# A second product in twenty block products instead of Strassen's seven, with PSUM in one-bank tiles and part of a convolution on ScalarE and GpSimd

## The chip, the cores and the metric

The kernel runs on one core of a Trainium2 chip. The metric is device time in microseconds, the median of several runs. PE is TensorE, DVE is VectorE, ACT is ScalarE, POOL is GpSimd, SP the queue that issues most DMAs.

## The reference

x has shape (8, 4096, 192). Each of 8 heads (24 channels) is filtered along the sequence by 7 causal taps, the softmax of `weight`. The result, 32,768 tokens by 192, goes through an MLP of 2048 hidden units, all in float32:

```python
out = np.einsum('hk,bskhg->bshg', w, x_unf)      # 7 taps, per head
h = out.reshape(B * S, D) @ w_in                 # 192 -> 2048
g = h * (1.0 / (1.0 + np.exp(-1.702 * h)))
y = g @ w_out                                    # 2048 -> 192
```

## The kernel before

Work goes in 32 chunks (`big`), each of 512 tokens from both halves of the batch, 1024 in all. Channels or hidden units lie on the partitions, tokens along the free dimension. Chunk 0 goes its own way in `first_step`, beside loading, splitting and rounding the weights (which arrive as float64 words). Every later chunk is one step of three parts:

- The convolution on DVE, two chunks ahead: `transpose_x` (L414) turns x, `conv` (L429, L431) applies seven taps for each of three groups of 64 channels (c = 0, 1, 2), and `sums_c` (L338, L340) forms eight sums. DMAs copy them to the other half of the partitions (`cross`, L440).
- The first product, `hidden`, once for v = 0 and once for v = 1: 21 terms each, every term two matmuls of 512 columns on two row tiles side by side (L492). DVE and ACT combine the partial sums in PSUM and in `room`, and ACT applies the activation into `g` (`gelu`, L509).
- The second product, `output`: Strassen's scheme in Winograd's form, seven products of halves. Five calls of `product2` each give three column tiles of 32 to a product and the fourth to a third of another one; `quarters` (L614) does what is left. A product sums over 8 blocks of 128 hidden units, in matmuls of 512 columns (L597). DVE forms the sums of halves of g (`sum_1` to `sum_4`, L512), adds the products (L671 to L708) and transposes back (`turn`, L632). `store` (L645) writes out.

The order is written out by hand. `prepare` lists the convolution's operations, each with a cost in microseconds; `work(us)` takes as many off the list as fit, `need(label)` takes all up to a label:

```python
def work(us):
    while todo and todo[0][1] <= us + 0.2:
        us -= todo[0][1]
        todo.pop(0)[2]()
```

Every engine runs its own instructions in that order, semaphores between them. PSUM is four tiles of two banks each (`slots`, `sums`).

Of the kernel before, what the change touches and what calls it, by code (L numbers as in the profile page):

```python
# [8 lines left out]
F32 = mybir.dt.float32  # L9
# [6 lines left out]
def kernel(  # L16
# [44 lines left out]
    NK = NF // 2  # L61
# [15 lines left out]
    xin_pool = ctx.enter_context(tc.tile_pool(name="xin", bufs=1))  # L77
# [7 lines left out]
    xins, xts = {}, {}  # L85

    def load_x(big, ns=range(2)):
# [3 lines left out]
        if big not in xins:  # L91
            xins[big] = xin_pool.tile([P, 2, NJ, XW], F32, name="xin")
            if c == 0:
                nc.gpsimd.memset(xins[big][0:R, :, 0, :], 0.0)  # L94
        xin = xins[big]
# [14 lines left out]
    slots = [psum.tile([P, 2, TOK], F32, name=f"slot{i}") for i in range(3)]  # L110
    sums = psum.tile([P, 2, TOK], F32, name="sums")
# [3 lines left out]
    B11, B12, B21, B22, T1, T2 = range(6)  # L115
    T3, T4 = B12, B21
    g = consts.tile([P, 4, NU, 2, 2, TOK], F32)
# [4 lines left out]
    k15, k20, k19, k18, k16 = (room[:, i, :].rearrange("p (h n) -> p h n", h=2) for i in range(5))  # L122
    u1, u2 = (room[0 : NC * Q, 4, i * TOK : (i + 1) * TOK] for i in range(2))
    osbs = consts.tile([P, 4 * TOK], F32)
    osb = osbs[0 : NC * Q, :].rearrange("q (n j e) -> q n j e", n=2, e=2 * Q)
    p3, p4 = (osb[:, n, :, Q : 2 * Q] for n in (1, 0))

    def half(b, u, cols, small):


        if small and b in (T1, T2):
            return room[:, 2 * (b - T1) + u, :].rearrange("p (v h t) -> p v h t", v=2, h=2)
        if b == T2:
            t = room[:, 2 * u : 2 * u + 2, :].rearrange("p v (h t) -> p v h t", h=2)
        else:
            t = g[:, B11 if b == T1 else b, u, :, :, :]
        return t[:, :, :, cols]

# [59 lines left out]
    NS = 7  # L200
    A11, A12, A21, A22, S1, S2, S4 = range(NS)
    S3 = A21
    w_out_s = consts.tile([P, NS, NK, HD], F32)

# [6 lines left out]
    assert PIECE == CW * D and 3 * PIECE <= NB * T and 3 * PIECE <= 2 * NJ * XW  # L211
    flat_room = room.rearrange("p i n -> p (i n)")
    places = w_in_s[:, 4 * NC : NA, :].rearrange("p a f -> p (a f)")
    b12, b22 = (g[:, b, 1, :, :, :].rearrange("p v h t -> p (v h t)") for b in (B12, B22))
# [13 lines left out]
    def scratch(flat):  # L228
# [6 lines left out]
        scratch(w_out_s[:, S1 : S4 + 1, :, :].rearrange("p i f d -> p (i f d)")),  # L235
# [100 lines left out]
    def add_up(v, dst, a, op, b):  # L336
        if op == "+":
            vec.tensor_add(v(dst), v(a), v(b))  # L338
        elif op == "-":
            vec.tensor_sub(v(dst), v(a), v(b))  # L340
        elif op == "n":
            vec.scalar_tensor_tensor(
                out=v(dst), in0=v(a), scalar=-1.0, in1=v(b), op0=ALU.mult, op1=ALU.subtract
            )
        else:
            vec.tensor_scalar_mul(v(dst), v(a), -1.0)
# [10 lines left out]
    def round_w_out(i):  # L357
        join_piece(NW + i)
        k, j = divmod(i * CW, NK)
        round_piece(  # L360
            NW + i,
            [
                (
                    lambda v, m=m: v.rearrange("p (b m d) -> p b m d", m=2, d=Q)[:, :, m, :],
                    w_out_s[:, 2 * m + k, j : j + CW, :].rearrange("p j (c d) -> p (j c) d", d=Q),
                )
                for m in range(2)
            ],
        )

    def sums_w_out():
        a = [w_out_s[:, i, :, :] for i in range(NS)]
        vec.tensor_add(a[S1], a[A21], a[A22])
        vec.tensor_sub(a[S2], a[S1], a[A11])
        vec.tensor_sub(a[S4], a[A12], a[S2])
# [9 lines left out]
    pw = slots[0][:, 0, 0 : NC * (K + 1)].rearrange("p (c k) -> p c k", c=NC)  # L385


    def begin_sums(js, dst=sums):
        for j in js:
            nc.tensor.matmul(  # L390
                dst[:, j // 4, j % 4 * P : (j % 4 + 1) * P],
# [543 lines left out]
```

## Time and profile before

| | |
|---|---|
| median of 3 runs | 2353.68 us (2353.04 to 2353.89) |
| profiled execution, span from first to last instruction | 2351.6 us |
| granted TensorE clock, mean | 0.999 |
| busy PE, DVE, ACT, POOL | 2343.7, 1951.7, 1018.4, 5.8 us |
| SP queue's share of 16 DMA engines | 27.5% |

The profiled execution's own time is known only as its span; 2.1 us lie between it and the median. The profile lists groups of instructions by source line, with count, total busy time, mean duration and the idle time ahead of them. In the timeline a row has the start, the duration, and the count of instructions merged into it.

### The profile page before, as it was taken

Reading aid. Unit: us, or ns where it says so; the run is one execution under the profiler, and the core shown is the slowest. Engines: PE = TensorE matmul, PEld = TensorE weight load, DVE = VectorE, ACT = ScalarE, POOL = GpSimd, SP = SyncE. Lnnn points to the kernel's source line nnn. Section 1 sums busy time; section 2 is a strip of 40 time slices with the busy share of each in tenths; the row PEclk is TensorE's granted clock in tenths of the full one; section 3 lists DMA queues with packets and bytes.
Section 4 is the critical chain, followed back from the end, with each engine's and each line's share of the span. In section 5 each row is a group of like instructions: output and inputs, shape, how many; then the busy total and the mean of one; then the engine's idle time right before and its main releaser. Section 6 shows DMA issues by size and latency. Waiting matters only on the chain.

```text
span 2351.6 us, 39193 instructions
## 1 busy us (share of the span) xinstructions
PE 2343.7 (100%) x16856; PEld 892.0 (38%) x16856; DVE 1951.7 (83%) x2186; ACT 1018.4 (43%) x1159; POOL 5.8 (0%) x23
## 2 busy tenths in 40 slices
PE   9999999999999999999999999999999999999998
PEld 5533333333333333333333333333333333333333
DVE  8988888888888888888888888888888888888866
ACT  7234543345533355433454334543345533345433
POOL 0000000000000000000000000000000000000000
PEclk9999999999999999999999999999999999999999
DMA  8323313323123232132331332312323223231010
GB/s 182 69 48 76 68 21 64 63 57 68 36 49 66 55 69 50 35 65 55 68 64 22 68 64 58 68 30 54 67 55 69 46 39 67 55 68 43 17 41 15
DMA packets 197484, 133.67 MB, mean 57 GB/s; under 512 B 108592, under 2 KB 187824, under 8 KB 193344
## 3 DMA queue, kind: packets, MB, share of 16 engines
q1 hardware_dynamic: 196448, 130.92, 27.5%
q8 instruction: 132, 2.16, 0.4%
q14 instruction: 40, 0.33, 0.0%
q10 hardware_dynamic: 832, 0.20, 0.0%
q0 software_dynamic: 32, 0.07, 0.0%
HBM read 53.15 MB, written 25.17 MB: 33 GB/s over the span
## 4 chain that ended last, share of the span: by engine, by line
PE 67%; issue 32%; DMA 0%; DVE 0%; POOL 0%; POOLq 0%; DVEq 0%
PE slot L492 24%; PE slot L597 22%; PE sums L492 11%; PE sums L597 9%; PE slot L614 1%; PE slot L740 0%; PE sums L390 0%; DMA conv_t<-conv_t 0%; DVE xt L414 0%; PE slot L401 0%; POOLq L930 0%; POOL xin L94 0%; PE slot L390 0%; POOL osbs masks.py:199 0%; POOL osbs masks.py:197 0%
## 5 line engine op out<-in xcount | busy, mean ns | idle before, releaser
L492 PE MATMUL slot<-conv_t,w_in_s 64*128 64x512 f32 x3740 | 851.8, 590 | 0.0
L597 PE MATMUL slot<-g,w_out_s 128*32 128x512 f32 (+2 forms) x6864 | 788.7, 568 | 0.0
L492 PEld LDWEIGHTS slot<-conv_t,w_in_s 64*128 64x128 f32 x3740 | 359.6, 187 | 446.8 <-issue 394.6
L431 DVE SCALAR_TENSOR_TENSOR conv_t<-xt,cw,conv_t 128x512 f32<-128x512 f32 (+1 forms) x576 | 424.8, 738 | 13.0
L597 PEld LDWEIGHTS slot<-g,w_out_s 128*32 128x32 f32 x6864 | 241.8, 110 | 455.9 <-issue 439.0
L492 PE MATMUL sums<-conv_t,w_in_s 64*128 64x512 f32 x1660 | 405.4, 592 | 0.0
L509 ACT ACTIVATE g<-room 128x1024 f32<-128x1024 f32 x310 | 321.1, 1058 | 97.5 <-DVE room L574 58.3
L597 PE MATMUL sums<-g,w_out_s 128*32 128x512 f32 (+1 forms) x2304 | 335.0, 587 | 0.0
L512 DVE TENSOR_TENSOR g<-g 128x2048 f32<-128x2048 f32 (+1 forms) x126 | 283.2, 2267 | 4.7 <-PE sums L597 2.4
L492 PEld LDWEIGHTS sums<-conv_t,w_in_s 64*128 64x128 f32 x1660 | 158.3, 187 | 202.9 <-issue 160.9
L509 ACT ACTIVATE g<-slot 128x1024 f32<-128x1024 f32 x167 | 169.4, 1016 | 88.7 <-PE slot L492 88.7
L597 PEld LDWEIGHTS sums<-g,w_out_s 128*32 128x32 f32 x2304 | 93.1, 110 | 152.7 <-issue 146.3
L512 DVE TENSOR_TENSOR room<-g 128x2048 f32<-128x2048 f32 (+1 forms) x64 | 144.6, 2259 | 4.3
L512 DVE TENSOR_TENSOR g<-room,g 128x2048 f32<-128x2048 f32 (+1 forms) x64 | 140.2, 2229 | 0.0
L685 ACT COPY osbs<-slot 32x512 f32<-32x512 f32 (+1 forms) x32 | 18.3, 572 | 251.6 <-PE slot L614 251.6
L597 PE MATMUL slot<-room,w_out_s 128*32 128x512 f32 (+1 forms) x816 | 112.9, 567 | 0.0
L597 PE MATMUL sums<-room,w_out_s 128*32 128x512 f32 x768 | 112.7, 592 | 0.0
L686 DVE TENSOR_TENSOR room<-room,slot 96x512 f32<-96x512 f32 (+1 forms) x32 | 21.6, 675 | 91.1 <-ACT osbs L685 91.1
L670 ACT COPY osbs<-slot 32x512 f32<-32x512 f32 (+1 forms) x32 | 18.4, 574 | 174.4 <-PE slot L597 174.4
L554 DVE TENSOR_TENSOR slot<-slot,room 128x1024 f32<-128x1024 f32 x62 | 75.4, 1216 | 10.8 <-ACT g L509 10.8
L566 DVE TENSOR_TENSOR room<-slot,room 128x1024 f32<-128x1024 f32 x62 | 75.9, 1225 | 6.8 <-DVE room L562 0.5
L574 DVE TENSOR_TENSOR room<-room,sums 128x1024 f32<-128x1024 f32 x31 | 37.8, 1221 | 48.4 <-PE sums L492 48.4
(151 smaller groups left out, 1522.1 us busy)
## 6 DMA issues: line engine op xcount, KB each, us to landing
xin<-in_x_dram SPq DMA_DIRECT2D x240, 180.0 KB, 5.6
conv_t<-conv_t SPq DMA_DIRECT2D x62, 512.0 KB, 4.5
out_dram<-osbs SPq DMA_DIRECT2D x180, 128.0 KB, 2.5
conv_t<-conv_t SPq DMA_DIRECT2D x62, 256.0 KB, 3.6
conv_t<-conv_t SPq DMA_DIRECT2D x62, 64.0 KB, 1.9
xin<-in_x_dram SPq DMA_DIRECT2D x16, 160.0 KB, 5.5
osbs<-in_moe_w_out_dram SPq DMA_DIRECT2D x2, 768.0 KB, 8.8
out_dram<-osbs SPq DMA_DIRECT2D x20, 64.0 KB, 1.8
```

Of the source, the lines that this page charges most:

```text
L431: vec.scalar_tensor_tensor(out=dst, in0=src, scalar=tap, in1=dst, op0=ALU.mult, op1=ALU.add)
L492: nc.tensor.matmul(slot[:, h, :], w_in_s[halves[h], a, v * P : (v + 1) * P], src, start=first, stop=True, skip_group_check=True,)
L509: act.activation(g[:, b, u, v, :, :], src, AF.Gelu_apprx_sigmoid)
L512: vec.tensor_sub(*(half(x, u, cols, small) for x in (dst, a, b)))
L554: vec.tensor_sub(x, z, k15)
L566: vec.tensor_sub(k19, z, k19)
L574: vec.tensor_add(k20, k20, sums)
L597: nc.tensor.matmul(dst[l * Q : (l + 1) * Q, :], w_out_s[:, a, j, c * Q : (c + 1) * Q], half(b, u, cols, small)[:, v, h, :], start=(first a ...
L614: nc.tensor.matmul(dst[l], w_out_s[:, a, j, c * Q : (c + 1) * Q], half(b, u, cols, small)[:, v, h, :], start=(i == 0), stop=(i == NK // 4 ...
L670: act.copy(chunk(v3, 1), blocks(p3c))
L685: act.copy(chunk(v4, 0), blocks(p4c))
L686: vec.tensor_add(v1, v2, p5)
```

## The change

The second product of a steady step is rewritten (`second` for `output`). w_out is seen as two halves of outputs (m) by three groups of five blocks of hidden units (r = 1, 2, 3) with one block left over; g as those groups by four groups of 256 tokens (j). The 2x3 by 3x4 block product is formed by 20 block products of five matmul rounds of 256 columns: 15 are written out as calls of `go`, on three column tiles; five run as "side products" on the fourth tile, which also takes two of the eight leftover blocks (`rest`); the other six are appended to calls of `go` (`left`). Twelve sums of blocks of w_out are formed once (`SUMS_O`, `w_form`); sums of blocks of g are formed by DVE in every step, five in `hidden` with v = 1 and eleven in `second`. Chunk 0 takes a plain product (`second_plain`) in place of half Strassen, half plain.

PSUM becomes eight tiles of one bank. Copies and sums of 1024 columns that touch it are cut in two (`copy2`, `sum2`; `gelu` too).

Of the convolution, channel group 0 leaves DVE from chunk 3 on, and for chunk 1: ACT multiplies each tap (`tap_times`), from the list `ready`, which `second` draws on from its 54th round in steps of four; GpSimd adds them (`add_tap`) and also does all of `sums_c`. The transposes of x and the next load move from the start of the convolution's list to the end of `hidden` with v = 0 (`turn_x`). The last chunk no longer has its last product cut in three, and all stores go through SP.

```diff
-    slots = [psum.tile([P, 2, TOK], F32, name=f"slot{i}") for i in range(3)]
-    sums = psum.tile([P, 2, TOK], F32, name="sums")
-    B11, B12, B21, B22, T1, T2 = range(6)
...
-    g = consts.tile([P, 4, NU, 2, 2, TOK], F32)
+    slots = [
+        [psum.tile([P, TOK], F32, name=f"slot{i}{h}") for h in range(2)] for i in range(3)
+    ]
+    sums = [psum.tile([P, TOK], F32, name=f"sums{h}") for h in range(2)]
+    B11, B12, B21, B22 = range(4)
+    PAIRS = [(0, 0), (1, 1), (1, 0), (0, 1)]
+    NS, ND = 3, 5
+    assert len(PAIRS) * 4 == NF == NS * ND + 1
+    g = consts.tile([P, 2, NF, TOK], F32)
+    ROW = {1: 2, 2: 0, 3: 1}
+    COL = {1: (0, 0), 2: (0, 1), 3: (1, 1), 4: (1, 0)}
+    def block(r, j):
+        n, o = COL[j]
+        i = ND * ROW[r]
+        return g[:, n, i : i + ND, o * T : (o + 1) * T]
+    def rest(j):
+        n, o = COL[j]
+        return g[:, n, NF - 1 :, o * T : (o + 1) * T]
...
+    BLK = ND * T
+    t_s = osbs[:, 0:BLK].rearrange("p (k t) -> p k t", k=ND)
+    spare = consts.tile([P, 3, T], F32)
+    t_a, t_8 = (
+        flat_room[:, i * BLK : (i + 1) * BLK].rearrange("p (k t) -> p k t", k=ND) for i in range(2)
+    )
...
     def round_w_out(i):
         join_piece(NW + i)
-        k, j = divmod(i * CW, NK)
-        round_piece(
-            NW + i,
-            [
-                (
-                    lambda v, m=m: v.rearrange("p (b m d) -> p b m d", m=2, d=Q)[:, :, m, :],
-                    w_out_s[:, 2 * m + k, j : j + CW, :].rearrange("p j (c d) -> p (j c) d", d=Q),
-                )
-                for m in range(2)
-            ],
-        )
...
+        pi = PAIRS.index(divmod(i, NU))
+        dsts = []
+        for m in range(2):
+            for v in range(2):
+                for h in range(2):
+                    dsts.append(
+                        (
...
+                            w_out_s[:, m, 2 * (pi + v * len(PAIRS)) + h, :].rearrange(
+                                "p (c d) -> p c d", d=Q
...
+        round_piece(NW + i, dsts)
...
+    taps = [block(1, 3)[:, 0:2, :], block(1, 3)[:, 2:4, :], block(3, 1)[:, 3:5, :]]
+    taps += [block(1, 4)[:, 0:2, :], block(1, 4)[:, 2:4, :], block(3, 3)[:, 3:5, :]]
...
+    def tap_times(big, k):
+        dst = tap_home(big, k) if k else own(big)[:, 0:2, :]
+        act.mul(dst, conv_src(big, 0, k), cw[:, 0, k : k + 1])
+    def add_tap(big, k):
+        dst = own(big)[:, 0:2, :]
+        nc.gpsimd.tensor_add(dst, dst, tap_home(big, k))
     def sums_c(big, i):
-        add_up(lambda j: own(big)[:, place(big, j), :], *SUMS_C[i])
+        add_up(
+            lambda j: own(big)[:, place(big, j), :],
+            *SUMS_C[i],
+                eng=nc.gpsimd,
+        )
...
     def prepare(big):
-        for c in range(NC):
-            yield "", 0.7, lambda c=c: transpose_x(big, c)
-        if big + 1 < N_BIG:
-            yield "", 0.0, lambda: load_x(big + 1)
         v1 = place(big, V1)
-        for c in (0, 2):
+        for c in (0, 2, 1) if big == 2 else (2, 1):
             for k in range(K):
                 yield "", 0.76 if k else 0.48, lambda c=c, k=k: conv(big, c, k)
-        yield "", 0.38, lambda: sums_c(big, 0)
+        yield f"done {big}", 0.0, lambda: need(f"taps {big}")
+        yield "", 0.0, lambda: sums_c(big, 0)
         yield f"first {big}", 0.0, lambda: cross_when(True, big, v1, v1 + 1)
-        for k in range(K):
-            yield "", 0.76 if k else 0.48, lambda k=k: conv(big, 1, k)
         yield "", 0.0, lambda: cross_when(False, big, 0, C31)
         for i in range(1, len(SUMS_C)):
...
+    def prepare_taps(big):
+        for k in (*range(1, K), 0):
+            yield "", 1.0, lambda k=k: tap_times(big, k)
+        for k in range(1, K):
+            yield "", 0.0, lambda k=k: add_tap(big, k)
+        yield f"taps {big}", 0.0, lambda: None
...
         pe(sums, 12)
-        act.copy(k15, sums)
+        copy2(k15, sums)
         pe(x, 5, 17)
...
         pe(y, 6, 14, first=True)
-        vec.tensor_sub(x, z, k15)
-        work(2.6)
+        sum2(vec.tensor_sub, x, z, k15)
+        if v:
+            vec.tensor_add(t_s, block(2, 1), block(2, 4))
+            vec.tensor_sub(block(2, 1), block(2, 1), block(3, 1))
+        work(2.6 if v else 1.2)
...
         work(1.2)
+        if not v and big + 2 < N_BIG:
+            need(f"done {big + 1}")
+            turn_x(big + 2)
         pe(sums, 3, 19)
         work(0.7)
-        vec.tensor_add(k18, k18, sums)
+        sum2(vec.tensor_add, k18, k18, sums)
+        if v:
+            vec.tensor_add(block(2, 3), block(2, 2), block(2, 3))
+            vec.tensor_sub(t_8, t_s, block(3, 1))
         return lambda: gelu(B12, 1, v, k18)
...
+    def second_plain(fetch):
+        tasks = [(slots[0][0], 0, 1), (slots[1][0], 1, 0), (slots[0][1], 0, 0)]
...
+        for i, (dst, m, n) in enumerate(tasks):
+            for k in range(NF):
+                for l in range(NC + 1):
+                    a, b, c = (m, n, l) if l < NC else (1, 1, i)
+                    nc.tensor.matmul(
...
+                if k % 2:
+                    next_tap()
+            work((11.0, 14.0, 8.6)[i])
+            if i == 1:
+                fetch()
...
+    LATE, EVERY = 54, 4
+    def second(big, bx, by, bs, vec_work, final):
+        n3 = NC * Q
+        (m1, sa), (m2, m3), (sb, sc) = bx, bs, by
...
+        side, rounds_done = [], [0]
+        def side_product(w, t, to, h=0, first=True):
+            for c, bank in enumerate((sa, sb, sc)):
+                dst = bank[n3:, h * T : (h + 1) * T]
+                for k in range(t.shape[1]):
+                    last = k == t.shape[1] - 1
+                    side.append((dst, w[:, k, chunk_cols(c)], t[:, k, :], first and k == 0, last and chunk(to, c)))
+        one = lambda m: w_out_s[:, m - 1, NF - 1 :, :]
+        side_product(w_part(2, 2), block(2, 4), s12)
+        side_product(form(F16), block(2, 2), s16)
+        side_product(one(2), rest(2), s22, first=False)
+        side_product(form(F16), block(2, 1), s17)
+        side_product(one(1), rest(1), s11, first=False)
+        side_product(form(F1), block(1, 2), s4)
+        side_product(form(F1), block(1, 1), s1v)
...
+        def go(bank, h, w, t, first=True, left=None):
+            dst = bank[0:n3, h * T : (h + 1) * T]
+            steps = [(w[:, k, :], t[:, k, :]) for k in range(ND)]
+            if left:
+                steps.append((w_out_s[:, left[0] - 1, NF - 1, :], rest(left[1])[:, 0, :]))
+            for k, (wk, tk) in enumerate(steps):
+                for c in range(NC):
+                    one_matmul(chunk(dst, c), wk[:, chunk_cols(c)], tk, first and k == 0, k == len(steps) - 1)
+                d, ws, ts, st, to = side.pop(0)
+                one_matmul(d, ws, ts, st, to is not False)
+                if to is not False:
+                    act.copy(to, d)
+                rounds_done[0] += 1
+                if rounds_done[0] >= LATE and rounds_done[0] % EVERY == LATE % EVERY:
+                    next_tap()
+            return dst
+        add, sub = vec.tensor_add, vec.tensor_sub
...
+        sub(block(3, 3), block(1, 3), block(3, 3))
+        p3 = go(m1, 0, form(F3), block(3, 1), left=(2, 1))
+        act.copy(s21, p3)
+        sub(block(1, 3), block(1, 3), block(1, 1))
+        sub(block(3, 1), block(3, 4), t_8)
+        p11 = go(m2, 0, form(F11), block(3, 2), left=(1, 2))
+        act.copy(sc12, p11)
+        sub(block(1, 2), block(1, 2), block(3, 2))
+        p2 = go(m3, 0, w_part(1, 2), t_a)
+        act.copy(s2, p2)
+        add(t_a, block(2, 2), t_a)
+        p19 = go(m2, 1, form(F19), block(2, 3), first=False, left=(2, 3))
+        act.copy(s23, p19)
+        vec_work(2.8)
+        p8 = go(m1, 0, form(F8), t_8)
+        sub(v8, p8, s12)
+        p10 = go(m2, 0, w_part(1, 3), block(3, 1), left=(1, 4))
+        sub(t_8, t_a, block(3, 2))
+        sub(s23, s23, s16)
+        add(s14, p10, v8)
+        sub(block(2, 2), block(1, 1), block(3, 3))
+        q13p = go(m3, 0, form(F13), t_a, first=False)
+        act.copy(q13, q13p)
+        sub(s23, s23, q13p)
+        add(block(3, 2), block(1, 2), block(1, 4))
+        sub(block(2, 4), block(2, 2), t_s)
+        p15 = go(m2, 1, form(F15), block(1, 3), first=False, left=(1, 3))
+        sub(t_8, t_8, block(3, 2))
+        add(s13, p15, s2)
+        p20 = go(m3, 1, w_part(2, 1), block(3, 3), first=False)
+        add(s23, s23, p20)
+        done(2, 3, s23)
+        p6 = go(m1, 0, w_part(1, 1), block(1, 4))
+        sub(s14, s14, s17)
+        add(s14, s14, p6)
+        done(1, 4, s14)
+        vec_work(0.6)
+        sub(block(3, 4), block(3, 4), block(3, 2))
+        u7 = go(m3, 1, form(N7), block(2, 2), first=False)
+        sub(s13, s13, u7)
+        vec_work(0.6)
+        w9 = go(m1, 0, form(N9), block(3, 2), first=False)
+        sub(s24, s12, w9)
+        vec_work(0.6)
+        p5 = go(m3, 1, form(F5), block(2, 4), first=False)
+        sub(s24, s24, s4)
+        add(u5, p5, v8)
+        final()
+        add(s21, s21, u5)
+        done(2, 1, s21)
+        add(s22, s22, s4)
+        sub(s11, s11, u5)
+        vec_work(0.6)
+        beta = go(m1, 0, form(N14), t_8, first=False)
+        add(q13, q13, beta)
+        sub(sc12, sc12, q13)
+        done(1, 2, sc12)
+        add(s22, s22, q13)
+        done(2, 2, s22)
+        p18 = go(sa, 0, w_part(2, 3), block(3, 4), left=(2, 4))
+        add(s24, s24, p18)
+        done(2, 4, s24)
+        add(s13, s13, s1v)
+        done(1, 3, s13)
+        store(big, slice(0, TOK // Q), 1)
+        add(s11, s11, s1v)
+        done(1, 1, s11)
+        store(big, slice(0, TOK // Q), 0)
...
+    def next_tap():
+        if ready:
+            ready.pop(0)[2]()
...
         give(False, big)
         if more:
-            act.copy(sums, z)
+            need(f"all {big + 1}")
+        need("forms")
         if big + 2 < N_BIG:
-            todo.extend(prepare(big + 2))
-        output(big, y, x, work, ends=() if more else (z, sums))
-        if more:
-            need(f"all {big + 1}")
+            begin(big + 2)
+        second(big, x, y, sums, work, lambda: copy2(sums, z) if more else None)
         x, z = z, x
```

## The prediction

> **What bounds the kernel now.** I read the engine totals and the clock first, then the waits of TensorE, then its timeline, and only then the other engines.
>
> ```profile
> PE 2343.7 (100%) x16856; PEld 892.0 (38%) x16856; DVE 1951.7 (83%) x2186; ACT 1018.4 (43%) x1159; POOL 5.8 (0%) x23
> PEclk9999999999999999999999999999999999999999
> ...
> PE sums L390 <- POOL osbs masks.py:199: 1.4, 1, 1.4
> ```
>
> The last line is the whole answer to "whom does PE wait for": 1.4 us, once, at the start. A busy PE need not be PE at its peak, so its start times are what counts:
>
> ```profile
> 135.49 7.07 PE L597 MATMUL sums<-g,w_out_s 128*32 128x512 f32 x64
> 142.38 7.05 PE L597 MATMUL slot<-g,w_out_s 128*32 128x512 f32 x64
> 149.24 0.61 PE L597 MATMUL sums<-room,w_out_s 128*32 128x512 f32 x3
> ...
> 59.05 27.83 PE L597 MATMUL slot<-g,w_out_s 128*32 128x256 f32 x512
> 86.70 0.39 PE L597 MATMUL slot<-room,w_out_s 128*32 128x256 f32 x3
> ```
>
> Each matmul leaves two records, and four matmuls on the four column tiles run side by side as one "round" of eight records. 64 records are 8 rounds: 142.38 to 149.24 is 6.86 us, 0.858 a round of 512 columns. 512 records of 256 columns are 64 rounds: 59.05 to 86.70 is 27.65 us, 0.432 a round. A 256-column round thus costs 0.003 more than half of a 512-column one: narrow tiles are nearly free. Starts are as regular all along, so PE streams columns without a gap, and time falls only with columns. The step repeats: products with room begin at 1077.76 and, two steps on, at 1222.63 in the chain that ended last, so 72.44 us a step.
>
> ```profile
> 1077.00:1149.50 72.50, 72.50 (x506) 26.93 (x504) 60.60 (x66) 31.31 (x36) 0.00 (x0) 1.00 0.28 56
> 1150.50:1187.00 36.50, 36.50 (x340) 11.11 (x334) 31.11 (x28) 6.00 (x9) 0.00 (x0) 1.00 0.38 74
> ```
>
> After the span come PE, PEld, DVE, ACT, POOL. DVE has 12 us free in a step and 5 in the second product (the second row), ACT 30 in the latter.
>
> **The change, part by part.** Durations are of the profiled execution, span 2351.6; the median time is 2.1 above it, which I keep.
>
> *PE, a steady step (31 of them).* Before: five `product2` of 8 rounds and `quarters` of 2, so 42 rounds x 0.858 = 36.03. After: 15 calls of `go` with 5 rounds, six of them with a sixth for the leftover block, 81 rounds x 0.432 = 34.99; the fourth tile of each round takes a side product, 81 too, so no round is extra. In columns 20,736 for 21,504. The first product keeps its 42 pairs, the switches of tiling stay two. Gain 1.04 a step, 32.3 in all, if nothing makes PE wait.
>
> *The first chunk.* Before it took 90 rounds x 0.432 = 38.9; `second_plain` has 48 of 512 columns, 41.2: +2.3. It also asks for the last piece of w_out earlier: its third round reads blocks of piece 3, formerly read in the second half. DVE rounds that piece here:
>
> ```profile
> 60.04 0.95 DVE L319 SCALAR_TENSOR_TENSOR w_out_s<-osbs,w_out_s 128x768 uint32<-128x768 uint32 x1
> 61.02 1.03 DVE L323 SCALAR_TENSOR_TENSOR w_out_s<-w_out_s 128x384 f32<-128x384 f32 x2
> ```
>
> Two writes of 384 become eight of 96. By 555 ns for 384, with about 0.15 fixed, one of 96 takes 0.25 and 0.17 start to start: 0.4 more a piece, 1.2 late from the three pieces ahead. The fifth write is what round three needs: 61.02 + 1.2 + 0.93 = 63.15, against PE at 59.05 + 1.72 = 60.77. DVE has no gap there from 36 us on, so +2.4. The twelve sums of w_out blocks (480 elements, 0.65 each, 7.8) take the place of four of 0.96, and chunk 2 alone keeps its full conv; both lie beside 41 us of PE, where DVE loses the sums of halves and twelve to fifteen operations of chunk 1: nothing.
>
> *The end.* Before, the last product is cut into 256 and 2 x 128 columns, stores go out on three queues, and last matmul (2345.1) to end is 6.5. After, p18 is followed by five additions and transposes of 0.42 to 0.44 (about 3.1 us to the last `turn`), and six stores on SP alone at about 0.5 each, 2.5 landing and 1.3 to the end (as after the last issue before): 9.0. With 0.3 less on PE, +2.2.
>
> *DVE.*
>
> ```profile
> L431 DVE SCALAR_TENSOR_TENSOR conv_t<-xt,cw,conv_t 128x512 f32<-128x512 f32 x558 | 416.1, 746 | 12.4
> L512 DVE TENSOR_TENSOR g<-g 128x2048 f32<-128x2048 f32 x124 | 280.8, 2284 | 4.7 <-PE sums L597 2.4 <-PE slot L597 2.4
> L554 DVE TENSOR_TENSOR slot<-slot,room 128x1024 f32<-128x1024 f32 x62 | 75.4, 1216 | 10.8 <-ACT g L509 10.8
> L686 DVE TENSOR_TENSOR room<-room,slot 96x512 f32<-96x512 f32 x31 | 21.2, 683 | 89.2 <-ACT osbs L685 89.2
> L340 DVE TENSOR_TENSOR conv_t<-conv_t 128x256 f32<-128x256 f32 x186 | 73.2, 421 | 3.2
> ```
>
> The rows give 1.04 ns an element and 0.15 fixed. Removed a step: seven taps of the conv (4.9), eight `sums_c` (3.4), eight sums of halves (18.2). Added: 16 block sums of 1,280 elements at 1.48 (23.7), 21 additions of 96x256 at 0.42 for the former eleven of 512 at 0.68 (+1.3), 8 short transposes for 4 long (+0.7), and the twelve 1024-wide sums cut in two (24 x 0.68, +1.8). About 64 for 60.6; start to start less, since independent neighbours overlap by 0.08. It fits 71.4, but not everywhere. A walk through the second product, PE at 0 with p3, DVE in its new order at 1.40 a block sum, 0.34 to 0.45 a small one, 0.79 a tap:
>
> - t_8 4.2 (p8 asks at 9.9); the new block (3,1) 8.4 (p10 at 12.1); t_a 11.2 (p13 at 14.7); after four taps of conv, block (2,2) 17.9 (u7 at 23.8); (3,2) 19.6 (w9 at 25.9); (2,4) 21.0 (p5 at 28.1); t_8 again 22.4 (beta at 30.2); (3,4) 27.1 (p18 at 32.4).
> - The reads that free a PSUM bank are closer: s23 has read p20 at 23.2, and u7 overwrites it at 23.8; s13 has read u7 at 27.5, p5 comes at 28.1.
>
> Every sum is ready, the thinnest margin 0.6 us. I cost it at nothing; the cover is that margin.
>
> *ACT.* Twelve copies of 1024 become 24 of 512; its row for 128x512 is 585 ns, so 1.07 a pair start to start for 1.01. PE's reuse of `sums` keeps about half a microsecond. 26 small copies (0.37) and seven taps (about 0.6) enter a second product with 30 us of idle ACT. Nothing.
>
> *GpSimd.* Six additions of 512 and eight of 256 a step. Its nearest row:
>
> ```profile
> L274 POOL TENSOR_TENSOR room<-osbs 128x64 f32<-128x64 f32 x1 | 0.3, 307 | 0.0
> ```
>
> At DVE's slope that is 0.77 and 0.51, 8.7 a step; at no fixed part at all (307/64 an element) 2.5 and 1.2, 25. The Trainium skill, "GPSIMD Engine Reference", 3.1, states about 2.6 cycles of 1.2 GHz an element for such an addition: with 0.17 fixed 1.28 and 0.72, an estimate of 13.4, which I take. It is late nowhere: the last tap ends near 34.3 of a second product, additions until 7 us into the next step, `sums_c` from the last conv at 17 to 23, V1 first; PE fetches with V1 at 33. At 25 us a step V1 still comes near 24.
>
> The rule that speaks against the change is in "SBUF — State Buffer", Who interferes with whom: a DVE instruction with two SBUF inputs and a GpSimd one that reads SBUF exclude each other for the whole instruction. The trace, with POOL idle, cannot show it. By the rows alone DVE pays 0. By the rule it pays up to 13.4 a step: 60 + 13.4 = 73.4, over the 71.4 of PE. I take 0 to 3: in 34 to 42 and 52 to 58 DVE mostly reads one operand from PSUM or transposes, where the rule does not bite, with only the last output sums, a tap or two and two block sums exposed. Their delay is covered by 2 to 4 us of idle DVE in each half of the first product.
>
> *DMA.* Stores, `load_x` and crossings keep their bytes. `load_x` (8 issues, 5.6 landing) moves half a step, ahead of the V1 crossing on SP, both needed 15 us or more later. Nothing.
>
> Sum: -32.3 + 2.3 + 2.4 + 2.2 = -25.4, less what bits of waiting come with thin margins (31 x 0 to 0.2). Span 2326, time 2328.
>
> **The rivals.**
>
> *The margins give way.* DVE is 0.6 to 1.6 late at u7 and p5, because of a slip in my walk or of port waits, and PE waits 0.5 to 1.0 a step: +15 to +31 us, 2343 to 2359. For it: 32 us of DVE work in 35. Against: the waits fall on two or three of fifteen products, and DVE's rows vary by 1%.
>
> *DVE becomes the bound through the shared port: slower.* Place: block sums and conv taps against the 14 additions of GpSimd. It decides once DVE loses over 11 us a step (71.4 less 60); at the full 13.4 a step is 73.4 to 74 against 72.44, 31 x 1.0 to 1.6 = +31 to +50, with the first chunk and end (+7) about 2390 to 2410. For it: the rule, and DVE at 85%. Against: GpSimd runs mostly where DVE reads PSUM.
>
> *The columns are not saved*, because 256-column rounds with output in two banks run slower than 0.432. At 0.445 the gain is gone: 31 x 81 x 0.013 = 33, about 2360. Against: 64 such rounds in a row at 0.432, and rounds with mixed operands from 86.70 on too.
>
> **How the numbers follow.** PE stays the bound: 0.68, 2322 to 2336, likeliest 2328. Margins give way: 0.19, of which two thirds still over 0.2% faster. Slower by the port: 0.08. Columns not saved or the unforeseen: 0.05. A measurement tells 0.2%, 4.7 us, from no change. Faster: 0.68 + 0.13 + 0.02 = 0.83; same 0.05; slower 0.12. The range takes the likeliest case and most of the second: 2320 to 2350; below 2320 PE has no columns left to lose.
>
> **What would show it.** Right: 256-column rounds at 0.432, a step of 71.4, PE's waits in the second product under 0.2 a step, one gap of 2 to 3 us near 61, a tail near 9. Wrong: u7, p5 or w9 waiting for DVE in every step; block sums or taps lengthened or preceded by gaps while POOL is busy; `fetch` waiting for a crossing or for POOL. A time over 2350 makes the walk wrong, one over 2365 the port estimate.

## The result and the profile after

The changed kernel takes 2325.47 us (median of four runs, 2325.26 to 2326.32), the kernel before beside it 2353.61 (four runs, 2353.04 to 2353.89): a ratio of 0.9881, 95% interval 0.9867 to 0.9895. The predicted time was 2328, in a range of 2320 to 2350. The profiled execution's span is 2324.6.

The lines are read in the order of the prediction. First the engine totals, the clock, and the waits of PE (engine, what it waited for; us in total, times, longest):

```profile
PE 2314.0 (100%) x26064; PEld 1224.9 (53%) x26064; DVE 1988.2 (86%) x2813; ACT 1367.4 (59%) x2526; POOL 428.1 (18%) x450
PEclk9999999999999999999999999999999999999999
...
PE sums L430 <- POOL osbs masks.py:199: 1.4, 1, 1.4
PE slot L678 <- issue: 1.3, 1, 1.3
```

POOL went from 6 to 428 us and ACT from 1018 to 1367, and still PE waits for nobody but at the start. The second wait is new and lies in the first chunk. Then the timeline of PE there, and of DVE's rounding of the last piece of `w_out`:

```profile
60.33 1.92 PE L678 MATMUL slot<-g,w_out_s 128*32 128x512 f32 x16
63.57 26.57 PE L678 MATMUL slot<-g,w_out_s 128*32 128x512 f32 x240 [1.32 <-issue]
...
63.21 1.44 DVE L361 SCALAR_TENSOR_TENSOR w_out_s<-w_form 128x96 f32<-128x96 f32 x8
```

Two rounds, then a gap of 1.5 us that ends 0.36 after the eight writes have begun: the third round reads that piece. Three of its column tiles go on after the first write; the fourth starts at 64.19, behind the fifth write (to 64.14), and stays behind the others. The view gives the releaser as "issue", so that it is this wait rests on an experiment below. Last, a steady step and, in the second row, a second product (span, then PE, PEld, DVE, ACT, POOL, the clock):

```profile
1033.00:1104.40 71.40, 71.40 (x822) 37.43 (x818) 61.63 (x86) 42.72 (x79) 13.87 (x15) 1.00 0.26 57
1069.00:1104.00 35.00, 35.00 (x646) 20.85 (x648) 33.35 (x47) 16.88 (x36) 0.45 (x1) 1.00 0.17 41
```

PE is busy from end to end of both, DVE has 1.65 us free in the second. From start to start of the second product it is 71.35 us in every steady step but the last, which fetches nothing for a next one and takes 70.49 (before: 72.44, in four steps 72.68 or 72.70, in the last 71.58).

The ledger, by the starts of the second product in the two traces. The first steady one comes at 141.69 (135.49 before): +6.2. From it to the last one it is 2139.7 (2173.3 before): -33.5. From the last one to the end 43.2 (42.9 before): +0.3. Sum -27.0, which is the difference of the spans, 2324.6 and 2351.6.

### The profile page after: what moved, and what is told of

The parts are those of the page before. It is cut to its first block, busy times and chain, and to the rows that moved or that the text cites. A ratio compares the mean times of both kernels' runs of the same rounds, so it can differ in the third digit from the quotient of the medians.

```text
span 2324.6 us, 60417 instructions
## 1 busy us (share of the span) xinstructions
PE 2314.0 (100%) x26064; PEld 1224.9 (53%) x26064; DVE 1988.2 (86%) x2813; ACT 1367.4 (59%) x2526; POOL 428.1 (18%) x450
## 4 chain that ended last, share of the span: by engine, by line
PE 100%; DVE 0%; issue 0%; POOL 0%; POOLq 0%
PE slot L553 35%; PE slot L749 33%; PE sums L553 15%; PE sums L749 14%; PE slot L678 2%; PE slot L878 0%; PE sums L430 0%; PE slot L441 0%; DVE osbs L704 0%; PE slot L430 0%; DVE spare L835 0%; DVE g L837 0%; DVE g L840 0%; POOL osbs masks.py:199 0%; POOL osbs masks.py:197 0%
## 5 line engine op out<-in xcount | busy, mean ns | idle before, releaser
L749 PE MATMUL slot<-g,w_form 128*32 128x256 f32 x6700 | 772.3, 379 | 0.0
L488 POOL TENSOR_TENSOR conv_t<-conv_t,g 128x512 f32<-128x512 f32 x174 | 234.7, 1349 | 1443.8 <-ACT conv_t L484 1432.4
L749 PEld LDWEIGHTS slot<-g,w_form 128*32 128x32 f32 x6700 | 399.3, 110 | 135.9 <-ACT g L574 22.7
L749 PE MATMUL sums<-g,w_form 128*32 128x256 f32 x3530 | 461.8, 379 | 0.0
L749 PE MATMUL slot<-g,w_out_s 128*32 128x256 f32 x4430 | 442.0, 379 | 0.0
L749 PEld LDWEIGHTS sums<-g,w_form 128*32 128x32 f32 x3530 | 233.3, 110 | 66.3
L583 ACT COPY room<-slot 128x512 f32<-128x512 f32 x434 | 231.4, 600 | 57.0 <-PE slot L553 57.0
L574 ACT ACTIVATE g<-slot 128x512 f32<-128x512 f32 x334 | 179.8, 591 | 86.5 <-PE slot L553 86.5
L749 PE MATMUL sums<-g,w_out_s 128*32 128x256 f32 x1708 | 205.8, 379 | 0.0
L749 PE MATMUL slot<-room,w_form 128*32 128x256 f32 x2340 | 182.1, 379 | 0.0
L587 DVE TENSOR_TENSOR room<-slot,room 128x512 f32<-128x512 f32 x248 | 156.2, 681 | 22.3 <-ACT room L583 22.3
L587 DVE TENSOR_TENSOR room<-room,sums 128x512 f32<-128x512 f32 x124 | 79.1, 678 | 68.2 <-PE sums L553 68.2
L587 DVE TENSOR_TENSOR room<-room,slot 128x512 f32<-128x512 f32 x124 | 79.1, 679 | 67.4 <-PE slot L553 67.4
```

What stands on the lines that cost most here:

```text
L488: nc.gpsimd.tensor_add(dst, dst, tap_home(big, k))
L574: act.activation(g[:, n, i + h, :], src[h], AF.Gelu_apprx_sigmoid)
L583: act.copy(bank(dst, h), bank(src, h))
L587: op(*(bank(t, h) for t in (dst, a, b)))
L749: nc.tensor.matmul(dst, w, t, start=first, stop=last, skip_group_check=True)
```

## Experiments

The theory is that time is TensorE's columns, so long as every read of a PSUM bank ends before PE comes back to that bank. The rivals are that VectorE's load, the port shared by VectorE and GpSimd, or the PSUM tiles do more than that. Times are medians of four runs each. In the three sets of runs the kernel before took 2352.9 to 2353.3.

**PSUM tiles of two banks.** The second product with the tiles as before:

```diff
-    slots = [[psum.tile([P, TOK], F32, name=f"slot{i}{h}") for h in range(2)] for i in range(3)]
-    sums = [psum.tile([P, TOK], F32, name=f"sums{h}") for h in range(2)]
+    pairs = [psum.tile([P, 2, TOK], F32, name=f"slot{i}") for i in range(4)]
+    slots = [[t[:, h, :] for h in range(2)] for t in pairs]
+    sums = slots.pop()
```

> The changed kernel with its eight one-bank PSUM tiles put back into four tiles of two banks, the products addressed as halves of them. Theory (time is TensorE's columns, and waits are set by regions, so a tile's size does not matter): 2325.5, within 0.2%, the step 71.35. Rival (a two-bank tile makes TensorE wait for the reader of the other bank too): in the second product several banks are read within 0.7 to 1.5 us of their next writer, so with a wait of 0.5 to 1.5 at four to six products a step it is 2 to 6 a step, 31 times: 2390 to 2510.

Measured: 2715.61 us, ratio to the kernel before 1.1541 (1.1523 to 1.1558). My theory fell, the rival was too small. The step is 83.94, 12.6 more. The waits of PE, the two largest of nine such rows:

```profile
PE slot L748 <- ACT spare L762: 39.3, 31, 1.3
PE slot L748 <- DVE g L802: 33.2, 31, 1.1
```

Each row comes once a step (one twice), and each names the reader of a product in the tile. The matmuls and the readers are the same as in the changed kernel, so a product waits for the readers of its whole tile, not of the region that it overwrites. The second row shows it: L802 is `add(s13, p15, s2)`, which reads p15 in m2; the product behind it, p20, writes m3, the other bank of the same tile. The nine rows add up to 6.4 of the 12.6 us a step, because a row counts from the modelled end of the matmul before; from start to start, the delays of the products in one second product (47.4 us long for 34.8) are the whole 12.6. In the trace each of these waits is for a semaphore: the program sets it by the tile. Between two banks the chip does not need it, since in the changed kernel p20 starts 2.9 us before that read of p15 begins; for two halves of one bank no run shows whether it does. The edit that looked like bookkeeping is thus what makes the rest of the change possible: with everything else in it, the kernel without it is 362 us slower than the kernel before.

**The sums of conv blocks back on VectorE.** `eng=nc.gpsimd` becomes `eng=vec` in `sums_c`:

> The changed kernel with the eight 256-column sums of conv blocks a step back on VectorE (about 8 x 0.42 = 3.4 us a step), GpSimd keeping only the additions of the conv. Theory (VectorE has idle time enough in the first product, where these sums lie): 2325.5, within 0.2%; step 71.35; GpSimd 7.5 busy a step. Rival (VectorE is nearly full, every microsecond shows): up to +3.4 a step, 2325 + 105 = 2430; a third of it if only part is exposed, 2360.

Measured: 2326.69 us, ratio 0.9888 (0.9872 to 0.9905). Step 71.35, its window:

```profile
1033.00:1104.35 71.35, 71.35 (x824) 37.57 (x816) 64.44 (x94) 42.72 (x79) 8.10 (x7) 1.00 0.26 57
```

DVE takes 2.8 us a step more, POOL 5.8 less, PE the same. The theory held: this part of the offload is worth nothing.

**No offload at all.** The conv's third group of taps goes back to VectorE as well:

```diff
-        for c in (0, 2, 1) if big == 2 else (2, 1):
+        for c in (0, 2, 1):
...
-        ready.extend(prepare_taps(big))
```

> The changed kernel with all of the conv and its sums back on VectorE: no work for GpSimd in a steady step, ScalarE loses its seven multiplications. VectorE gets about 7 x 0.75 + 8 x 0.42 = 8.6 us a step more, less 2.0 a step that the overlap with GpSimd now costs it: 61.6 + 6.6 = 68.2 of 71.35. Theory 1 (a total under the step is not enough; seven conv operations that found no place at the start come in one go at the end of the first half of the step, and the second product's margins of 0.5 to 0.7 us are thin): TensorE waits 0.5 to 3 us a step, 2340 to 2420. Theory 2 (only the total counts): 2325.5 within 0.2%. Theory 3 (the offload costs more through the shared port than it takes off): faster, 2318 or less.

Measured: 2515.43 us, ratio 1.0689 (1.0673 to 1.0705); a step of 76.8 to 78.5. The direction of theory 1, at twice its upper size. DVE just ahead of where PE stops, in one step (timeline), and the waits of PE:

```profile
2301.99 4.69 DVE L477 SCALAR_TENSOR_TENSOR conv_t<-xt,cw,conv_t 128x512 f32<-128x512 f32 x6
...
2309.49 1.28 DVE L587 TENSOR_TENSOR room<-room,sums 128x512 f32<-128x512 f32 x2
...
PE sums L553 <- DVE room L587: 49.3, 15, 3.3
PE slot L553 <- DVE room L587: 47.5, 15, 3.4
```

Six leftover taps (4.69), three transposes of the next input (2.10) and two sums of conv blocks (0.84, these in the lines left out), 7.6 us, stand ahead of the pair L587 that frees PE's bank. In the steady steps PE's next matmul comes 3.5 us late. DVE is busy 86% of the whole: not its total binds, but what is queued ahead of one read. The other half of the loss was not foreseen. The clock in the stretch with the wait and in the one after it:

```profile
2306.00:2310.50 4.50, 1.17 (x7) 0.34 (x4) 4.43 (x8) 2.05 (x4) 0.00 (x0) 0.93 0.03 8
2310.50:2317.00 6.50, 6.50 (x17) 4.68 (x19) 6.40 (x11) 2.23 (x3) 0.00 (x0) 0.52 0.06 14
```

The third number from the end is the granted clock: 0.52 for 6.5 us after the wait, some 3 us lost, and 1.00 before and later. Of the 190 us above the changed kernel, the waits are 97 by their two rows, and most of the rest is this.

**The offload alone, in the kernel before.** Its second product and PSUM tiles stay; `sums_c` and a third of the conv's additions go to GpSimd, the multiplications for them to ScalarE:

> The kernel before, its second product untouched (20 Strassen-type half products of 512 columns), with only the offload of the change: the eight conv-block sums and a third of the conv's additions on GpSimd, the multiplications for them on ScalarE. Theory (before, TensorE had no wait but one of 1.4 us in the whole span, so VectorE's load was not what set the time): 2353.6, within 0.2%, step 72.44. Rival 1 (the offload brings part of the gain): as low as 2335. Rival 2 (exclusion between VectorE and GpSimd makes VectorE late, its sums of 2048 elements being the longest that can be blocked): 13 us of GpSimd a step, 1 to 3 us a step on TensorE, 2385 to 2445.

Measured: 2372.3 us, ratio 1.0082 (1.0067 to 1.0097). The steady step is 72.65 for 72.44: no gain from freeing VectorE, as the theory said. The loss of 19 was not in it. Some 11 of it are in the first chunk, 8.2 of these one wait of PE for a ScalarE copy; I put that down to how I set the offload into that chunk's order, which no run tests. About 6 are the 0.2 a step. In every step one VectorE operation has grown, the last addition of the outputs: it has both inputs in SBUF and meets a GpSimd sum of conv blocks. An addition just ahead of it, with one operand in PSUM, has not (mean ns after the bar and busy us):

```profile
L721 DVE TENSOR_TENSOR room<-room,osbs 96x512 f32<-96x512 f32 x30 | 26.3, 876 | 0.0
...
L719 DVE TENSOR_TENSOR room<-room,slot 96x512 f32<-96x512 f32 x15 | 10.2, 677 | 0.0
```

In the kernel before they take 645 and 677. What follows on VectorE, and the ScalarE copy behind it, end 0.24 us later, and PE, which waits for that copy, loses 0.2: the exclusion of rival 2, at a fifth of its size or less. The other groups show who gives way (the second is the longest sum):

```profile
L431 DVE SCALAR_TENSOR_TENSOR conv_t<-xt,cw,conv_t 128x512 f32<-128x512 f32 x372 | 337.9, 908 | 7.8
L525 DVE TENSOR_TENSOR g<-g 128x2048 f32<-128x2048 f32 x124 | 280.5, 2282 | 4.7 <-PE sums L610 2.4 <-PE slot L610 2.4
...
L446 POOL TENSOR_TENSOR conv_t<-conv_t,taps 128x512 f32<-128x512 f32 x186 | 534.0, 2871 | 938.5 <-ACT conv_t L442 926.4
```

GpSimd's addition takes 2871 ns for 1349 in the changed kernel, DVE's long sum 2282 as without GpSimd, DVE's taps 908 for 746. Here it is mostly GpSimd that waits.

**GpSimd in the second product.** Useless additions where the changed kernel has almost none. In the second line of the diff the count is 4, then 2 and 6:

```diff
+            act.copy(load, w_out_s[n3:, 0, 0:5, :])
+            for _ in range(4):
+                nc.gpsimd.tensor_add(load, load, w_out_s[n3:, 0, 0:5, :])
```

> The changed kernel with four useless GpSimd additions of 480 columns (32 partitions, two inputs in SBUF, about 1.27 us each, 5.1 a step) put into 30 of the 31 second products, set going by one small ScalarE copy about 10 us after its start, where VectorE has 33 of 35 us filled and reads mostly SBUF. Theory (VectorE's instructions with two SBUF inputs and GpSimd's exclude each other for their whole length; the prediction's margin of 0.5 to 0.7 us is what hides it): VectorE loses 2.5 to 5 us a step there, TensorE waits 2 to 4.5 at u7, p5 or w9, 30 times: 2385 to 2460, and block sums of 1.40 show lengths up to 2.7. Rival (engines share SBUF without harm, the longer operations of the profile have another reason): 2325.5 within 0.2%.

Measured: 2433.05 us, ratio 1.0339 (1.0324 to 1.0355). VectorE and PE lose what the theory said. In the timeline of one second product (start, us):

```profile
2255.44 6.34 POOL L792 TENSOR_TENSOR room<-room,w_out_s 32x480 f32<-32x480 f32 x4 [26.51 <-ACT room L790]
2255.89 4.83 DVE L477 SCALAR_TENSOR_TENSOR conv_t<-xt,cw,conv_t 128x512 f32<-128x512 f32 x3
2260.64 0.41 DVE L795 TENSOR_TENSOR room<-slot,room 96x256 f32<-96x256 f32 x1
2260.98 2.15 DVE L797 TENSOR_TENSOR room<-room,g 128x1280 f32<-128x1280 f32 x1
```

Three taps take 4.83 where the changed kernel has 2.33 (1.48 for a block sum, here 2.15); L795, with one operand in PSUM, keeps its 0.41. DVE loses 3.2 us to four additions, PE waits 2.85 a step. But it waits at `p15`, not at u7, p5 or w9 as I had written. Steps are 74.24 (71.35 and the wait) and 75.9, mostly in turn; in the latter the clock fell to half for 3.4 us, which was not in the theory.

> The run with useless GpSimd additions in the second product, two instead of four (30 steps). With four, VectorE lost 3.2 us beside them, TensorE waited 2.85 at p15, and in every second step the clock then fell to half for about 3.4 us. Theory (each GpSimd addition holds up one VectorE instruction by about 0.8; the clock falls only after waits of near 3 us and more): loss 1.7, wait 1.3 at p15, granted clock 0.999, every step alike at 72.7: 2325.5 + 30 x 1.3 = 2365. Rival (every wait costs clock): 74 or more, 2400. Rival 2 (margin larger than thought): 2325.5.

Measured: 2365.37 us, ratio 1.0052 (1.0037 to 1.0067); step 72.72, PE's wait at `p15` 1.34, clock 0.999 throughout. As the theory said.

> The same with six useless GpSimd additions (30 steps). Theory (0.8 lost on VectorE for each, and a wait over about 3 us puts TensorE at half clock for some 3.4 us or twice that, in every step): wait about 4.5, then 2 to 4 us lost by the slower clock, step 78 to 80, 2325.5 + 30 x 6.5 to 8.5 = 2520 to 2580. Rival (only the wait counts, the clock's fall has another cause): 2325.5 + 30 x 4.5 = 2460, clock as in the changed kernel.

Measured: 2477.84 us, ratio 1.0530 (1.0513 to 1.0548). The wait is 3.86. Only five of the six additions end before VectorE has read p10, and each has cost it 0.85 us (0.86 with two, 0.81 with four, the margin of 0.37 counted in). The sixth starts beside that read and is held up itself, by the four block sums that follow, each at its usual 1.48:

```profile
927.70 7.54 POOL L792 TENSOR_TENSOR room<-room,w_out_s 32x480 f32<-32x480 f32 x1
```

The clock falls, but not in every step and by less than I expected: steps are 75.24, which is the wait alone, or 76.6 to 76.9 (one 78.15). After the longest waits seen here, 2.85 to 3.9 us, the loss by the clock was thus 0 to 3.6 us a step; after 1.3 and 1.4 none. So the length of a wait alone does not decide. The traces record when the granted clock changes: in each of the thirteen these times are whole multiples of 3.413 us apart, whatever the program does, and half clock lasts one to three such windows. Cut by these windows, two waits of 2.85 us in the run with four additions look like this (window, span, PE's busy time, the clock behind the bracket):

```profile
983.17:986.58 3.41, 1.42 (x28) 1.00 0.00 0
986.58:990.00 3.42, 2.73 (x52) 1.00 0.00 0
...
1058.26:1061.68 3.42, 0.74 (x16) 1.00 0.00 0
1061.68:1065.09 3.41, 3.41 (x36) 0.50 0.00 0
```

The first wait is split over two windows, with 2.0 and 0.7 us of idle PE, and costs no clock; the second leaves PE idle for 2.7 in one window, and the next one runs at half clock. It is the same in all the traces: the 70 windows at full clock that a half-clock one follows have 1.97 us or more of idle PE (by the modelled ends of its matmuls), the 8879 others 2.05 or less. So what costs clock is about 2 us of idle PE, 60% of a window, inside one window; a wait of 2.85 us is long enough for it, but only where the windows do not halve it. When half clock ends after one window and when after more, these figures do not settle. The Trainium skill, "TensorE: Matmul & The Clock Gate", What's actually happening, puts the clock down to activity in a window of about 3.4 us that runs free of the kernel, and the traces agree. It has the clock fall after an idle window; here 2 us of idleness in one were enough.

**Fewer columns.** Without the leftover block's products in the steady steps (in the lines left out ScalarE's taps also start in the 48th round for the 54th):

```diff
-        side_product(one(2), rest(2), s22, first=False)
-        p3 = go(m1, 0, form(F3), block(3, 1), left=(2, 1))
+        p3 = go(m1, 0, form(F3), block(3, 1))
...
```

> The changed kernel without the leftover block's products (six rounds of main products and their six side products of 81 rounds a step are left out, so the output lacks these terms; the first chunk keeps all of its rounds). Theory (columns bind, but the margins in the second product are 0.7 and 0.5 us): up to u7 four rounds fewer, 1.73 us, up to p5 also 1.73, so TensorE arrives 1.06 and 1.2 us before VectorE is done at u7 and p5; it waits about 1.2 there, and the step is 71.35 - 2.59 + 1.2 = 69.96: 2325.5 - 31 x 1.39 = 2282. Rival 1 (TensorE's columns alone): 6 x 0.432 = 2.59 a step, 2325.5 - 80 = 2245. Rival 2 (VectorE already binds): 2325, no gain.

Measured: 2289.53 us, ratio 0.9730 (0.9714 to 0.9746). Columns bind, and a margin gives way at once: the step is 70.31, 1.04 less for 2.59 of columns. The size was near, the place again wrong (the step was put at 69.96, with waits at u7 and p5). One of two rows of the waits, the other being the same for the tile `sums` in every second step:

```profile
PE slot L747 <- DVE room L792: 17.9, 15, 1.2
```

L792 here is `add(s14, p10, v8)`, and the product that waits is `p15`. It writes the second half of the bank whose first half holds p10. Set beside the two-bank run: the wait is for the whole tile, even where that is one bank. The same place in the changed kernel, DVE's read and PE's first `p15` matmul (timeline):

```profile
1085.35 0.41 DVE L794 TENSOR_TENSOR room<-sums,room 96x256 f32<-96x256 f32 x1
...
1086.14 0.39 PE L749 MATMUL sums<-g,w_form 128*32 128x256 f32 x3
```

L794 ends at 1085.76, PE comes at 1086.14: 0.38 of margin, thinner than any that the prediction listed. By this reading, moving that addition ahead of two others should end the wait:

```diff
+        add(s14, p10, v8)
         sub(t_8, t_a, block(3, 2))
         sub(s23, s23, s16)
-        add(s14, p10, v8)
```

> The run without the leftover block's products again (the same terms are left out of the output), with one thing moved: the addition that reads p10 goes ahead of the two VectorE operations (1.4 and 0.34) that stood before it. In that run TensorE waited 1.4 us a step at p15, which writes the other half of the bank that this addition reads. Theory (the wait is for that one reading, by the whole bank): it is done 1.74 earlier, 14.75 after the start of the second product, ahead of p15 at 15.1; the wait at p15 goes, and the next margin decides: u7 comes at 22.0, while s23 has read p20 at 23.1, so 1.0 is waited there; step 70.31 - 1.40 + 1.05 = 69.96, time 2289.5 - 31 x 0.35 = 2279. Rival 1 (p15 waits for its operands or for VectorE as a whole): 2289.5 as without the move. Rival 2 (no further margin): 2246.

Measured: 2297.85 us, ratio 0.9766 (0.9751 to 0.9780), step 70.54: slower than without the move. The waits, again without the rows for `sums`:

```profile
PE slot L747 <- DVE room L796: 14.8, 15, 1.1
...
PE slot L747 <- DVE room L803: 5.3, 16, 0.3
```

The wait at `p15` is gone, so the reading of it was right; that the next margin is u7 was not. L796 is `sub(s23, s23, q13p)`, which reads q13p in the other half of the bank that `p20` writes. PE comes there at 17.3 after the start of the second product, and that read ends at 18.4, so PE waits 1.1; then u7 waits 0.3 for L803, the read of p20. The margins lie one behind the other, and to move a read forward at the first leaves the next where it was. The sum of the waits is even 0.2 longer than before the move. The moved addition reads `v8`, which the operation just ahead of it writes; the trace gives that one as its releaser, and it starts 0.13 after its end (14.54 for 14.41), where independent neighbours overlap by 0.08. So every read behind it comes 0.2 later (that of q13p ends at 18.43 for 18.21).

**The first chunk's gap, and the end.**

```diff
+        ORDER = [0, 1, *range(4, 10), *range(12, NF), 2, 3, 10, 11]
-            for k in range(NF):
+            for at_k, k in enumerate(ORDER):
```

> The changed kernel with one thing different in the first chunk: the second product visits the blocks of the last piece of the output weights as its last four rounds of each task, not as third, fourth, eleventh and twelfth. Theory (the gap of about 1.5 us near 62 us is the wait for VectorE's rounding of that piece): the gap goes, 2325.5 - 1.5 = 2324.0, every later row 1.5 earlier. Rival (what is late is something else on VectorE or ScalarE, or the time comes back later since the next step starts on data that come no earlier): 2325.5, gap elsewhere.

Measured: 2323.16 us (2323.13 to 2323.61), ratio 0.9873 (0.9858 to 0.9887); its profiled span is 2321.9. PE's timeline shows no gap:

```profile
59.43 27.68 PE L679 MATMUL slot<-g,w_out_s 128*32 128x512 f32 x256
```

From its start to the next product the first chunk's second product takes 42.5 us for 44.7 in the changed kernel, 2.1 less, so it was the wait for the last piece: 1.5 in the gap, the rest in the fourth tile that came after the others. In the first product that follows 0.4 of it are lost again (37.1 for 36.7). The start is 0.9 earlier too, which the edit does not touch: the time at which the steady steps begin varies between the profiles of these kernels by up to 1.6 us. The kernel with this edit is the fastest of those that compute everything. Its advantage of 2.3 us over the changed kernel is between two sets of runs, and their ratios' intervals overlap; what carries it is the 2.1 of the two timelines, of which 1.7 remain at the first steady second product.

```diff
+                q = act if big == N_BIG - 1 and (c + n) % 2 else nc.sync
+                q.dma_start(out=rows[c], in_=osb[c * Q : (c + 1) * Q, n, js, :])
```

> The changed kernel with the last chunk's six stores a half shared between SP's and ScalarE's queues, three each, where all were issued by SP. Theory (of the 5.4 us between the last transpose and the end of the span about 1.5 is six issues one after the other on SP, at 0.5 each): three issues fewer on the path, 2325.5 - 1.0 = 2324.5, tail 4.4. Rival (the end is set by the landing of the last store and not by its issue, or ScalarE's issue is slower): 2325.5, tail 5.4.

Measured: 2326.06 us, ratio 0.9884 (0.9869 to 0.9899), the span 2324.7 for 2324.6: the rival. In the DMA views the median from issue to landing is 2.6 us for six stores on SP in the changed kernel, and 3.5 for three each on SP and ScalarE here. Issuing takes 2.13 us for 3.27, but each store takes 0.9 longer to land: the end follows the landing of the stores, not SP's issues. Why they take longer to land no run shows.

## Why the prediction was right, point by point

- *Columns*, -32.3 predicted: right. 256-column rounds start 0.432 apart (two passes of 0.216), and 15 products with 81 rounds take 35.0. The step went from 72.44 to 71.35, 1.09 for 1.04.
- *PE waits for nobody*: right, but "the thinnest margin 0.6" was not. The two listed margins were well found, u7 0.68, p5 0.82 and in one step 0.50. The walk followed reads and writes of the same half-bank and so passed over `p15`, which has 0.38, and `p20`, which has 1.2. The run with fewer columns and the GpSimd runs all stop at `p15` first. The forecast stood because that margin held, not because it was known.
- *DVE's order*: right to 0.2. The block sums were done at 8.5, 11.3, 17.9, 19.6, 21.0, 22.4 and 26.9 after p3, for 8.4, 11.2, 17.9, 19.6, 21.0, 22.4 and 27.1. Its total was added up wrongly: the terms listed give 61.6 a step, not "about 64". Measured are 61.6, 2.0 of them by the port, so 59.6 without it, against the 60 that the prediction went on with.
- *GpSimd*, 13.4 a step: 13.87 measured, by 1349 ns for 512 columns and 736 for 256 (1.28 and 0.72 by the estimate), the first lengthened in part by VectorE.
- *The port*, "I take 0 to 3": about 2.0. The rule of the Trainium skill in "SBUF — State Buffer", Who interferes with whom, agrees with the rows: two DVE additions of 96x256 with both inputs in SBUF meet GpSimd and take 1038 and 966 ns on average (0.38 us in the last second product, where GpSimd is idle), and the one with an operand in PSUM stays at 417:

```profile
L837 DVE TENSOR_TENSOR g<-g,spare 96x256 f32<-96x256 f32 x31 | 32.2, 1038 | 0.0
...
L835 DVE TENSOR_TENSOR spare<-spare,slot 96x256 f32<-96x256 f32 x31 | 12.9, 417 | 12.2 <-PE sums L749 6.3 <-PE slot L749 5.9
```

  PE pays nothing for it, since nearly all of it falls into the first product. The GpSimd runs show the price where that isn't so: 40 us in all for two additions a step.
- *The first chunk*, +4.7: the columns were 2.3 as predicted (42.5 without the gap, 40.2 before), the wait for the last piece 2.1 for 2.4. It was the fifth write that the last tile waited for, as predicted. Another 1.3 came ahead of the chunk (60.33 for 59.05) and 0.5 in the first product behind it, neither forecast; with 59.43 in the run that only moves the piece, most of the 1.3 looks like the spread from profile to profile.
- *The end*, +2.2: PE's last matmul starts at 2316.3, 8.2 before the end of the span, 6.8 before the change: +1.4 for the +2.5 that the tail alone was given. Its terms add up to 9.9, not 9.0; from the end of the last matmul it is 7.9. The term mis-sized is the stores: six issues were counted one after the other behind the last `turn` (3.0), but two of them start before it ends, and the last one 1.9 behind it. The additions and transposes took 2.5 for 3.1, the landing 2.6 for 2.5, the rest 0.9 for 1.3.
- *PSUM in one-bank tiles* was costed at 24 ScalarE copies for 12, as a side matter. It is the condition for all else.

## What to carry to other kernels

When PE goes round a few PSUM banks, list for every product which reads of the same tile, whatever part of it, must end first, and give each its margin: one-bank tiles were worth 12.6 us a step here, and the first two margins to break were reads of the other half of a bank. Where a product set is made shorter, see that the reads come forward with it: of 2.59 us of columns taken away, 1.04 came through. Place GpSimd additions where VectorE reads PSUM or transposes; fourteen a step cost TensorE nothing there, while each costs VectorE 0.8 to 0.9 us where it reads two operands from SBUF, and TensorE as much once the margin is gone.

## What the runs showed of the hardware

The clock: a window of 3.413 us with about 2 us or more of idle PE was followed by one to three windows of half speed (a pass every 0.427 us for 0.216), so that waits of 2.85 to 3.86 us cost up to twice their length or nothing beyond it, by where the windows cut them; many waits of up to 1.9 us, ten and more a step in the two-bank run, left the clock at 0.999. GpSimd and VectorE hold each other up in both directions: GpSimd's addition took 2871 ns beside sums of 2282, and a tap of VectorE in the changed kernel takes 750 ns without an addition beside it, 1450 with one (29 taps).
